# Attention values: rows that neighbouring spans share are loaded once and copied on the chip by GpSimd

## The chip, the cores and the metric

The kernel runs on one core of a Trainium2 chip. A core has five engines with a queue each: TensorE (PE in the profile, its weight loads PEld), VectorE (DVE), ScalarE (ACT), GpSimd (POOL) and SyncE (SP). They run side by side, each takes its own instructions in order, and they wait for one another through semaphores. Sixteen DMA engines move data between the memory of the chip (DRAM) and the core's own memory (SBUF); matmuls write to PSUM. The metric is the device time of one execution in microseconds (us).

## The reference

The program is three layers for 3072 tokens of width 512: chunked attention, a mixture of eight experts of which each token uses two, and a layer that takes the elementwise maximum of three products. Only the first is touched. Per head, it is:

```python
chunk, left_ctx, right_ctx = (32, 16, 8)          # B=4, H=8, S=768, D=64, 8 memory rows
for c in range(S // chunk):
    c_start, c_end = c * chunk, c * chunk + chunk
    k_ctx = k[:, :, max(0, c_start - 16):min(S, c_end + 8)]
    v_ctx = v[:, :, max(0, c_start - 16):min(S, c_end + 8)]
    k_full = np.concatenate([mem_k, k_ctx], axis=2)
    v_full = np.concatenate([mem_v, v_ctx], axis=2)
    scores = scale * np.matmul(q_c, k_full.transpose(0, 1, 3, 2))
    a = np.exp(scores - np.max(scores, axis=-1, keepdims=True))
    a = a / (np.sum(a, axis=-1, keepdims=True) + 1e-09)
    out[:, :, c_start:c_end] = np.matmul(a, v_full)
```

A chunk of 32 queries sees 56 rows of k and v (16 before, its own 32, 8 after) and 8 memory rows. The spans of two neighbouring chunks start 32 rows apart, so they share 24 rows.

## The kernel before

The 3072 tokens are 24 tiles of 128, six for each of the four batches; tile t holds four chunks c. The heads go in four pairs pr. For each tile, v is laid out for the matmul as `vbs[t % NV]` with NV = 3 buffers: partitions 0 to 63 (index a = 0) hold the window of the even head of a pair, partitions 64 to 127 (a = 1) that of the odd head, 56 rows of v and 8 memory rows each; the free dimensions are pair, chunk, and 64 values with a one behind them (D + 1 = 65, so that the product also gives the sum of the weights). The halves of the buffer that belong to the other head are set to zero once, by `clear`. The layout in DRAM (`vw`) is made by `_layout` on the host and has every span in full: a row that two spans share stands there twice.

`load_v(t)` fills the buffer of tile t with two DMAs of the SP queue, one for each a, of 64 rows (56 where the memory rows still stand in the buffer from the tile three before) of 4160 bytes.

The stage runs in steps, written out by `step(t)` for t from -2 to 23. A step holds, in the order in which the engines get them: on even t `load(t + 6)` (k and q of two tiles, from the ACT queue once t + 6 is 6 or more); `scores(t + 2)` on PE; `pv(t)`, the 16 products with v (32 rows of the profile) into `po`; `shift(t + 2)` on DVE (line 369 the maximum, line 372 the subtraction); `expo(t + 2)` on ACT (line 375); `windows(t + 4)`, which spreads k into its spans with two ACT copies (lines 345 and 346) and on two tiles of each batch with two POOL copies (line 350); `ptrans(t + 1)` on PE and its ACT copy (line 383); `xtrans(t - 1)` and its ACT copy (line 409); `gate`; `norm(t)` on DVE with the store of x to `xd` from the SP queue (line 401); and then `load_v(t + 3)` on SP (line 334). So a tile of v is asked for when the product that last read its buffer and the store of that step have been given out, and is used three steps later.

Between these, `pump` deals out the instructions of `route`, the routing of tokens to experts, for groups of tiles. For the first three groups two of its operations run on POOL (lines 444 and 445); DVE takes them up at line 449. At the end of the third group `unit_fetch` lets POOL fetch the first rows for the experts (line 264). From step 19 on, the weights of the experts are split as well (`wsplit`, ACT line 216 and DVE line 213). After step 23 the experts' matmuls begin, which run to the end of the program.

Of the kernel before, what the change touches and what calls it, by code (L numbers as in the profile page):

```python
# [8 lines left out]
F32 = mybir.dt.float32  # L9
# [10 lines left out]
B, H, S, D = 4, 8, 768, 64  # L20
N, DM = B * S, H * D
E, F = 8, 1024
F2 = 768
NT = N // 128
TB = S // 128
HP = H // 2
W = 64
# [9 lines left out]
NV = 3  # L37
# [13 lines left out]
def tile_kernel(ctx, tc, qT, kT, mkT, vw, wgn, noise, w1, w2, m2w, out):  # L51
    nc = tc.nc
    PE, ACT, DVE, POOL, SP = nc.tensor, nc.scalar, nc.vector, nc.gpsimd, nc.sync
# [17 lines left out]
    ld = passing.enter_context(tc.tile_pool(name="ld", bufs=3, side="right"))  # L71
# [14 lines left out]
    def psum(kind, which=None):  # L86
        if which is not None:
            return turns_[kind][which]
        taken[kind] += 1
        return turns_[kind][(taken[kind] - 1) % len(turns_[kind])]  # L90

    def mm(o, l, r, start=True, stop=True):
        PE.matmul(o, l, r, start=start, stop=stop)  # L93

    def spin(o, n, joined=False):

        for i in range(n):
            if n == 10:
                mm(o, ones_r[:, 0:128], ones_r[:, 0:512], start=not joined or i == 0, stop=not joined or i == n - 1)
            else:  # L100
                mm(o, ones, warm, start=(i == 0), stop=(i == n - 1))
# [182 lines left out]
    for e in range(E):  # L284
        n = 512 if e else U0
# [16 lines left out]
    z_all = rt.tile([128, NT, 16], F32, name="z_all")  # L302

    kws = [wk.tile([128, 2, HP, 4, W], F32, name=f"kw{i}", bufs=1) for i in range(2)]
    vbs = [ld.tile([128, 2, HP, 4, D + 1], F32, name=f"v{i}", bufs=1) for i in range(NV)]
    lo, hi = slice(0, 64), slice(64, 128)

    def clear():
# [5 lines left out]
    def load(t):  # L314
        b, i = divmod(t, TB)
        if i == 0:
            m_t[b] = ld.tile([128, HP, 8], F32, name="mk", bufs=2)
            SP.dma_start(m_t[b], mkT[b])
        if i % 2 == 0:
            eng = SP if t < 6 else ACT  # L320
            k_t[t] = ld.tile([128, HP, 280], F32, name="k")
            q_t[t] = ld.tile([128, 2, HP, 128], F32, name="q")
            for j in range(2) if t == 0 else [slice(0, 2)]:
                ks = slice(0, 280) if t else slice(152 * j, 152 + 128 * j)
                eng.dma_start(k_t[t][:, :, ks], kT[b, i // 2, :, :, ks])
                eng.dma_start(q_t[t][:, j], qT[b, i // 2, :, j])
            k_t[t + 1], q_t[t + 1] = k_t[t], q_t[t]

    def load_v(t):
        b, i = divmod(t, TB)  # L330
        n = W if i < NV else 56
        for a in range(2):
            p = slice(64 * a, 64 * a + n)
            SP.dma_start(vbs[t % NV][p, a], vw[b, i, p])

    def windows(t):
        kw = kws[t % 2]
# [14 lines left out]
    sc_t, pp_t, pt_t, po_t, xp_t = {}, {}, {}, {}, {}  # L352
# [32 lines left out]
    def pv(t, pr):  # L385
        if pr == 0:
            po_t[t] = po_b
        o = 2 * (D + 1) * (pr % 2)
        for c in range(4):
            mm(po_t[t][32 * c:32 * c + 32, pr // 2, o:o + 2 * (D + 1)],  # L390
               pt_t[t][:, pr, 32 * c:32 * c + 32], vbs[t % NV][:, :, pr, c, :])

    def norm(t):
        pov = po_t.pop(t)[:, :, 0:4 * (D + 1)].rearrange("p a (h d) -> p a h d", h=4)
# [156 lines left out]
    def pump(n, tensor=True):  # L551

        for r in routes:
            r[1] -= 1
        moved = 1
        while n > 0 and moved:
            moved = 0
            for r in routes[:]:
                if n and r[1] <= 0 and (r[2] not in ("rank", "count", "table") or tensor) and (
                        r[2] != "rank" or r[3] == ranked[0]) and (r[2] != "table" or r is routes[0]):  # L560
                    r[2] = next(r[0], "end")
                    n, moved = n - 1, 1
                    if r[2] == "end":
                        routes.remove(r)
                    elif r[2]:
                        r[1] = hold[0]
# [5 lines left out]
    spin(idle, 12)  # L572
    consts(wk.tile([128, 128], F32, name="dif", bufs=1))
    load_v(0)
    load(2)
    windows(0)
    windows(1)
    clear()
    load_v(1)
    load_v(2)  # L580
    load(4)
    if NV == 4:
# [3 lines left out]
    def turns_of_first():  # L586
        if 0 in fetched:
            turned[0] += 1
            if turned[0] > UH:
                unit_turn(0, turned[1])  # L590
                turned[1] += 1

    def do(f, u, *pr):
        if 0 <= u < NT:
            f(u, *pr)

    def pairs(f, t):
        for pr in range(HP):
            do(f, t, pr)

    def step(t):
        if t + 6 < NT and t % 2 == 0 and t >= 0:
            load(t + 6)
        pairs(scores, t + 2)
        if t <= 0:
            spin(idle, 10 if t < 0 else 6, t == -1)
        pairs(pv, t)
        do(shift, t + 2)
        do(expo, t + 2)
        do(windows, t + 4)  # L610
        pairs(ptrans, t + 1)
        if t < NT - 2:
            pairs(xtrans, t - 1)
            pairs(gate, t - 2)
        turns_of_first()
        pump(PU[1], False)
        do(norm, t)
        if t == NT - 2:
            pairs(gate, t - 2)
            pairs(xtrans, t - 1)  # L620
        if t >= 0:
            do(load_v, t + NV)
        if t < NT - 2:
            pump(PU[2], False)
        else:
            pump(PL)
# [13 lines left out]
    for t in range(-2, NT):  # L640
        step(t)
        if t == WL:
            for _ in range(3):
                wload()
        if t >= WS:
            wsplit(DVE)
        turns_of_first()
# [194 lines left out]
    i = 40  # L842
# [31 lines left out]
    def second(xT, dst, step=lambda s: None, middle=lambda s: None, along=[]):  # L874

        h = [big.tile([128, 2, 512], F32R, name=f"h{i}") for i in range(6)]
        for f in range(3):
            ms = big.tile([128, 2, 512], F32, name=f"h{6 + f % 2}")
            for w in range(3):
                l = quads.pop(3 * f + w)  # L880
                for r in range(2):
# [12 lines left out]
                    if w == 2:  # L894
                        split(m, h[2 * f + r][:, 0, :], h[2 * f + r][:, 1, :], DVE)
        step(18)
        side = spread(along, 24)
        side[4].insert(0, partial(middle, 19))
# [155 lines left out]
    with tc.If(most > CAP):  # L1054
# [10 lines left out]
        with tc.For_i(0, NT // 4, 1) as b:  # L1065
# [3 lines left out]
            for j in range(4):  # L1069
                g = made["cv"].tile([128, 512], F32, name="sq", bufs=1)  # L1070
                SP.dma_start(g, xd[bass.ds(b * 512 + 128 * j, 128), :])
                p = psum("t").rearrange("p (k n) -> p k n", k=HP)
# [4 lines left out]
            for e in range(E):  # L1077
                yp = [misc, tabp, po_b[:, 0], po_b[:, 1]]
                for f in range(8):
# [4 lines left out]
                    p = psum("p")  # L1084
# [17 lines left out]


_INS = [("qT", (B, TB // 2, 128, 2, HP, 128)), ("kT", (B, TB // 2, 128, HP, 280)), ("mkT", (B, 128, HP, 8)),
        ("vw", (B, TB, 128, HP, 4, D + 1)), ("wgn", (DM, 16)), ("noise", (128, NT, E)),
        ("w1", (E, DM, F)), ("w2", (E, F, DM)), ("m2w", (12, 128, 1024))]


def _layout(q, k, v, mem_k, mem_v, moe_w_gate, moe_w_noise, moe_noise, moe_w1, moe_w2,
            moe2_w1, moe2_w2, moe2_w3, moe2_w_out):  # L1110
    import numpy as np
    f = np.float32
    qT = q.reshape(B, HP, 2, TB // 2, 2, 128, D).transpose(0, 3, 2, 6, 4, 1, 5)
    kp = np.zeros((B, H, S + 24, D), f)
    kp[:, :, 16:16 + S] = k
    vp = np.zeros((B, H, S + 24, D), f)
    vp[:, :, 16:16 + S] = v
    kT = np.stack([kp[:, :, 256 * i:256 * i + 280] for i in range(TB // 2)], 1)
    kT = kT.reshape(B, TB // 2, HP, 2, 280, D).transpose(0, 1, 3, 5, 2, 4)
    mkT = mem_k.reshape(B, HP, 2, 8, D).transpose(0, 2, 4, 1, 3)  # L1120
    vw = np.ones((B, TB, 4, HP, 2, W, D + 1), f)
    for i in range(TB):
        for c in range(4):
            o = 128 * i + 32 * c
            vw[:, i, c, :, :, 0:56, 0:D] = vp[:, :, o:o + 56].reshape(B, HP, 2, 56, D)
            vw[:, i, c, :, :, 56:64, 0:D] = mem_v.reshape(B, HP, 2, 8, D)
    vw = vw.transpose(0, 1, 4, 5, 3, 2, 6)
    wgn = np.concatenate([moe_w_gate, moe_w_noise], 1)
    nz = moe_noise.reshape(NT, 128, E).transpose(1, 0, 2)
    wi = np.stack([moe2_w1, moe2_w2, moe2_w3]).reshape(3, 2, 2, 128, 2, 3, 128).transpose(3, 5, 0, 2, 4, 1, 6)  # L1130
    wi = wi.reshape(128, 18, 4, 128)[:, :, [0, 1, 3, 2]]
    wo = moe2_w_out.reshape(2, 3, 128, DM).transpose(2, 1, 0, 3)
    m2w = np.concatenate([wi.reshape(128, 9216), wo.reshape(128, 3072)], 1)
    m2w = np.ascontiguousarray(m2w.reshape(128, 12, 1024).transpose(1, 0, 2)).view(np.int64)
    r = dict(qT=qT.reshape(B, TB // 2, 128, 2, HP, 128), kT=kT.reshape(B, TB // 2, 128, HP, 280),
             mkT=mkT.reshape(B, 128, HP, 8), vw=vw.reshape(B, TB, 128, HP, 4, D + 1), wgn=wgn,
             noise=nz, w1=moe_w1, w2=moe_w2, m2w=m2w)
    return {n: np.ascontiguousarray(r[n]) for n, _ in _INS}

# [14 lines left out]
```

## Time and profile before

| | us |
|---|---|
| median of 3 executions | 1147.58 (1144.96 to 1149.05) |
| the profiled execution | 1145.96 |
| its span, first to last instruction | 1144.1 |
| PE busy in the span | 1106.0 (97%) |
| DVE busy | 632.1 (55%) |
| ACT busy | 391.8 (34%) |
| POOL busy | 215.0 (19%) |

The profile is of one execution. A row names the line of the kernel, the engine, the operation, what it writes and reads, and how often; an idle time is put down to what ended it. PE being busy is a modelled figure, since matmuls are pipelined. The attention takes about the first 135 us of the span; what follows is bound by PE.

### The profile page before, as it was taken

What the parts mean: (1) busy time and instruction counts of PE and PEld (TensorE: products, weight loads), DVE (VectorE), ACT (ScalarE), POOL (GpSimd) and SP (SyncE); (2) the same over time, 40 slices, a digit from 0 to 9 for tenths busy, and PEclk for the clock granted to TensorE, in tenths of its full rate; (3) what the DMA queues carried; (4) which work ended last, traced back from release to release, by engine and by line L of the source; (5) the groups of instructions that cost most, each with busy time, mean ns of one, the idle gap of its engine ahead of it and who ended that gap; (6) DMA issues with size and microseconds to landing.
All of it is one profiled execution on the core that took longest, in us unless ns stands there. A gap on an engine that the chain in (4) does not pass through costs nothing. (4 is left out here: it accounts for less than half of the span.)

```text
span 1144.1 us, 17322 instructions
## 1 busy us (share of the span) xinstructions
PE 1106.0 (97%) x6803; PEld 927.5 (81%) x6804; DVE 632.1 (55%) x1258; ACT 391.8 (34%) x680; POOL 215.0 (19%) x237
## 2 busy tenths in 40 slices
PE   7888899999999999999999999999999999999997
PEld 4777788889888898888888887888877878887886
DVE  4587864363564645755646656334766585655221
ACT  5778423332422523424224332222411152113110
POOL 2001020000011001000110020233456524433000
PEclk9999899999999999999999999999999999999999
DMA  8999533361473544745735675484576635658301
GB/s 242 288 282 302 177 124 107 119 225 62 126 229 111 174 149 142 236 137 167 238 109 162 216 215 183 128 242 158 157 228 218 201 117 170 201 172 281 124 1 40
DMA packets 113689, 199.06 MB, mean 174 GB/s; under 512 B 8576, under 2 KB 46592, under 8 KB 113600
## 3 DMA queue, kind: packets, MB, share of 16 engines
q1 hardware_dynamic: 76736, 109.86, 30.5%
q0 software_dynamic: 34272, 78.13, 22.4%
q10 hardware_dynamic: 2592, 9.88, 2.7%
q8 instruction: 56, 0.92, 0.3%
q14 instruction: 33, 0.27, 0.1%
HBM read 151.18 MB, written 46.66 MB: 173 GB/s over the span
## 5 line engine op out<-in xcount | busy, mean ns | idle before, releaser
L93 PE MATMUL sc<-xT,w 128*128 128x512 f32 (+3 forms) x912 | 193.0, 358 | 5.2 <-DVE h L811 3.8
L93 PE MATMUL pp<-xT,w 128*128 128x512 f32 (+3 forms) x912 | 190.4, 356 | 0.0
L93 PEld LDWEIGHTS sc<-xT,w 128*128 128x128 f32 x912 | 157.0, 188 | 29.0 <-DVE xT L194 3.4
L93 PEld LDWEIGHTS pp<-xT,w 128*128 128x128 f32 x912 | 157.5, 188 | 19.3
L264 POOL DMA_INDIRECT g<-xd,tok x56 | 55.1, 984 | 525.4 <-PE idle L271 242.4
L93 PE MATMUL po<-w,h 128*128 128x512 f32 x548 | 135.0, 395 | 0.0
L93 PE MATMUL misc<-w,h 128*128 128x512 f32 x522 | 127.8, 394 | 0.0
L93 PE MATMUL tabp<-w,h 128*128 128x512 f32 x498 | 121.5, 394 | 0.0
L93 PEld LDWEIGHTS po<-w,h 128*128 128x128 f32 x548 | 101.1, 188 | 20.5
L93 PEld LDWEIGHTS misc<-w,h 128*128 128x128 f32 x522 | 96.5, 188 | 19.8
L93 PEld LDWEIGHTS tabp<-w,h 128*128 128x128 f32 x498 | 92.2, 188 | 18.9
L811 DVE SCALAR_TENSOR_TENSOR h<-sc,h 128x256 fp32r<-128x256 f32 (+2 forms) x96 | 39.8, 443 | 89.0 <-ACT h L807 89.0
L213 DVE TENSOR_TENSOR w<-st,w 128x1024 fp32r<-128x1024 f32 x67 | 81.0, 1217 | 12.5 <-ACT w L216 12.5
L811 DVE SCALAR_TENSOR_TENSOR h<-pp,h 128x256 fp32r<-128x256 f32 (+2 forms) x96 | 39.8, 443 | 72.7 <-ACT h L807 72.7
L807 ACT ACTIVATE h<-sc 128x512 fp32r<-128x512 f32 (+3 forms) x64 | 33.1, 517 | 113.3 <-PE sc L93 106.2
L216 ACT CAST w<-st 128x1024 fp32r<-128x1024 f32 x67 | 70.1, 1047 | 4.1 <-DMA st<-in_w 3.7
L264 POOL DMA_INDIRECT g<-ys,rows x48 | 49.6, 1033 | 102.3 <-DMA ys<-y 62.0
L807 ACT ACTIVATE h<-pp 128x512 fp32r<-128x512 f32 (+3 forms) x64 | 33.1, 517 | 77.5 <-PE pp L93 74.6
L251 ACT CAST top<-val 128x1024 fp32r<-128x1024 f32 x18 | 18.9, 1050 | 79.5 <-DVE val L246 62.7
L194 DVE TENSOR_TENSOR xT<-xp,xT 128x512 fp32r<-128x512 f32 (+1 forms) x35 | 23.3, 665 | 36.5 <-ACT xT L193 36.4
L93 PE MATMUL po<-v,pt 128*32 128x130 f32 x768 | 27.6, 286 | 15.0 <-ACT pt L383 9.3
L193 ACT CAST h<-h 128x128 fp32r<-128x128 f32 (+1 forms) x60 | 18.2, 363 | 66.8 <-DVE h L893 51.7
(197 smaller groups left out, 1571.7 us busy)
## 6 DMA issues: line engine op xcount, KB each, us to landing
st<-in_w SPq DMA_DIRECT2D x64, 512.0 KB, 3.5
w<-m2s POOLq DMA_DIRECT2D x27, 1024.0 KB, 8.2
ys<-y SPq DMA_DIRECT2D x48, 256.0 KB, 3.9
st<-in_m2w SPq DMA_DIRECT2D x24, 512.0 KB, 3.7
m2s<-top SPq DMA_DIRECT2D x18, 512.0 KB, 3.9
m2s<-val SPq DMA_DIRECT2D x18, 512.0 KB
xT<-m2s POOLq DMA_DIRECT2D x9, 1024.0 KB, 6.1
w<-m2s POOLq DMA_DIRECT2D x9, 768.0 KB, 6.7
```

The lines of the kernel that those rows point to most:

```text
L93: PE.matmul(o, l, r, start=start, stop=stop)
L193: ACT.copy(hi, src)
L194: (eng or POOL).tensor_tensor(lo, src, hi.bitcast(F32), op=ALU.subtract)
L213: (eng or POOL).tensor_tensor(w[:, 1, :], st, w[:, 0, :].bitcast(F32), op=ALU.subtract)
L216: return [n, lambda eng: ACT.copy(w[:, 0, :], st), low]
L251: ACT.copy(hi[0], full)
L264: POOL.indirect_dma_start(out=g[0:n], out_offset=None, in_=src, in_offset=bass.IndirectOffsetOnAxis(ap=idx, axis=0))
L807: ACT.activation(h[:, 0, 0:n], p[:, 0:n], AF.Relu)
L811: DVE.scalar_tensor_tensor(o[:, c], p[:, c], 0.0, h[:, 0, c].bitcast(F32), op0=ALU.max, op1=ALU.subtract)
```

## The change

The layout of v becomes chunk first: `vbs` and `vw` have the chunk ahead of the pair. `load_v` now brings rows 0 to 31 of a window for all four chunks, rows 32 to 55 for the last chunk alone, and the memory rows 56 to 63 for all four where they are needed: three DMAs for each a (two where the memory rows stand). A new function `overlap(t)` has POOL copy, for each a, rows 0 to 23 of chunks 1 to 3 to rows 32 to 55 of chunks 0 to 2: 24 partitions of 780 values. It is given out for tile t + 1 at the start of step t, behind `load` and ahead of `scores(t + 2)`. `pv` reads the same values by the new indices.

```diff
-    vbs = [ld.tile([128, 2, HP, 4, D + 1], F32, name=f"v{i}", bufs=1) for i in range(NV)]
+    vbs = [ld.tile([128, 2, 4, HP, D + 1], F32, name=f"v{i}", bufs=1) for i in range(NV)]
...
     def load_v(t):
         b, i = divmod(t, TB)
-        n = W if i < NV else 56
         for a in range(2):
-            p = slice(64 * a, 64 * a + n)
-            SP.dma_start(vbs[t % NV][p, a], vw[b, i, p])
+            for o, n, c in ((0, 32, slice(0, 4)), (32, 24, slice(3, 4)), (56, 8, slice(0, 4)))[0:3 if i < NV else 2]:
+                p = slice(64 * a + o, 64 * a + o + n)
+                SP.dma_start(vbs[t % NV][p, a, c], vw[b, i, p, c])
+
+    def overlap(t):
+
+        for a in range(2):
+            v = vbs[t % NV]
+            POOL.tensor_copy(v[64 * a + 32:64 * a + 56, a, 0:3], v[64 * a:64 * a + 24, a, 1:4])
...
-               pt_t[t][:, pr, 32 * c:32 * c + 32], vbs[t % NV][:, :, pr, c, :])
+               pt_t[t][:, pr, 32 * c:32 * c + 32], vbs[t % NV][:, :, c, pr, :])
...
     def step(t):
         if t + 6 < NT and t % 2 == 0 and t >= 0:
             load(t + 6)
+        do(overlap, t + 1)
         pairs(scores, t + 2)
...
-        ("vw", (B, TB, 128, HP, 4, D + 1)), ("wgn", (DM, 16)), ("noise", (128, NT, E)),
+        ("vw", (B, TB, 128, 4, HP, D + 1)), ("wgn", (DM, 16)), ("noise", (128, NT, E)),
...
-    vw = vw.transpose(0, 1, 4, 5, 3, 2, 6)
+    vw = vw.transpose(0, 1, 4, 5, 2, 3, 6)
```

## Rows read from the trace of the kernel before

**Rows 1.** Busy time by stretch: PE, PEld, DVE, ACT, POOL, granted clock, DMA share, GB/s.

```profile
40.00:60.00 20.00, 18.05 (x375) 16.39 (x368) 11.63 (x29) 16.12 (x26) 1.09 (x4) 1.00 1.00 309
...
120.00:140.00 20.00, 17.89 (x183) 15.87 (x176) 16.88 (x60) 9.68 (x18) 0.00 (x0) 0.86 0.52 165
140.00:1144.00 1004.00, 988.54 (x4755) 828.33 (x4754) 538.08 (x974) 295.82 (x530) 198.18 (x195) 1.00 0.52 162
```

**Rows 2.** PE's waits from 35 to 135 us: total us, times, longest us.

```profile
PE po L93 <- ACT pt L383: 9.3, 10, 1.4
PE po L93 <- DMA v<-in_vw: 1.8, 1, 1.8
```

**Rows 3.** The products with v of tiles 3, 6, 9, 12, 15, 18 (timeline).

```profile
35.17 1.09 PE L93 MATMUL po<-v,pt 128*32 128x130 f32 x32 [0.96 <-ACT pt L383]
...
47.77 1.07 PE L93 MATMUL po<-v,pt 128*32 128x130 f32 x32
...
61.70 1.09 PE L93 MATMUL po<-v,pt 128*32 128x130 f32 x32 [1.42 <-ACT pt L383]
...
75.35 1.09 PE L93 MATMUL po<-v,pt 128*32 128x130 f32 x32 [0.86 <-ACT pt L383]
...
89.10 1.09 PE L93 MATMUL po<-v,pt 128*32 128x130 f32 x32 [0.80 <-ACT pt L383]
...
102.42 1.09 PE L93 MATMUL po<-v,pt 128*32 128x130 f32 x32
```

**Rows 4.** DMA of the stretch 35 to 110 us; issues end with us to landing.

```profile
DMA packets 7653, 22.18 MB, mean 296 GB/s; under 512 B 1326, under 2 KB 1326, under 8 KB 7638
...
v<-in_vw SPq DMA_DIRECT2D x18, 260.0 KB, 7.9
...
k<-in_kT ACTq DMA_DIRECT2D x7, 560.0 KB, 5.9
```

**Rows 5.** The same of the stretch 0 to 400 us: stores of x, loads of q.

```profile
xd<-x SPq DMA_DIRECT2D x24, 256.0 KB, 3.3
...
q<-in_qT ACTq DMA_DIRECT2D x9, 512.0 KB, 6.5
```

**Rows 6.** SP's issues (timeline): first v, last q from SP, v after tile 6.

```profile
4.87 1.15 SPq L334 DMA_DIRECT2D v<-in_vw  x2
...
12.29 0.33 SPq L326 DMA_DIRECT2D q<-in_qT  x1
...
51.00 1.82 SPq L334 DMA_DIRECT2D v<-in_vw  x2
```

**Rows 7.** SP's own waits from 0 to 140 us: total, times, longest.

```profile
SPq L334 <- DMA q<-in_qT: 2.0, 3, 1.1
SPq L326 <- DMA v<-in_vw: 1.2, 1, 1.2
```

**Rows 8.** The issues of v, and ACT's stop before a load of q.

```profile
L334 SPq DMA_DIRECT2D v<-in_vw x48: 314/465/1577, 4.9 to 119.4; - x48
...
L326 ACTq EVENT_SEMAPHORE  x1: 2085/2085/2085, 14.9 to 14.9; - x1
```

**Rows 9.** POOL's operations by form: times, busy us, mean ns.

```profile
L350 POOL COPY kw<-mk 64x128 f32<-64x128 f32 x16 | 4.6, 288 | 35.9 <-PE sc L93 35.0 <-DMA mk<-in_mkT 0.3
...
L311 POOL MEMSET v<- 64x1040 f32 x3 | 2.9, 959 | 0.2
```

**Rows 10.** Routing between POOL and DVE, first and third group (timeline).

```profile
58.13 0.28 POOL L444 TENSOR_TENSOR a<-a,nz 128x48 f32<-128x48 f32 x1 [23.12 <-ACT a L440]
...
58.81 0.31 DVE L449 MAX8 top<-a 128x8 f32<-128x8 f32 x3 [0.22 <-POOL a L445]
...
91.20 0.62 DVE L424 TENSOR_TENSOR rc<-iota_j,co 128x448 f16<-128x448 f16 x1
...
91.43 0.48 POOL L444 TENSOR_TENSOR a<-a,nz 128x24 f32<-128x24 f32 x1 [2.41 <-DVE a L442]
```

**Rows 11.** ACT's later wait for k at the start (timeline).

```profile
23.19 0.94 ACT L345 COPY kw<-k 64x896 f32<-64x896 f32 x1 [3.12 <-DMA k<-in_kT]
```

More of the change, by code (lines that the diff above doesn't have):

```diff
@@ L1135, in _layout @@
     r = dict(qT=qT.reshape(B, TB // 2, 128, 2, HP, 128), kT=kT.reshape(B, TB // 2, 128, HP, 280),
-             mkT=mkT.reshape(B, 128, HP, 8), vw=vw.reshape(B, TB, 128, HP, 4, D + 1), wgn=wgn,
+             mkT=mkT.reshape(B, 128, HP, 8), vw=vw.reshape(B, TB, 128, 4, HP, D + 1), wgn=wgn,
              noise=nz, w1=moe_w1, w2=moe_w2, m2w=m2w)
```

## The prediction

> **What bounds the kernel now.** I read the stretches first [rows 1]. From 140 us on PE is busy for 988.5 of 1004 us, and the change touches nothing there: what it gains or costs must show as an earlier or later start of that part, so only the first 135 us count. There the DMA engines look full (share 1.00 at 309 GB/s from 40 to 60 us), which invites the reading that v's bytes set the pace. The second view, PE's waits [rows 2], says otherwise: in 100 us PE waited 9.3 us for the transposed weights from ACT and once, 1.8 us, for v. The pace is a loop through PE, DVE and ACT, three steps of which take 12.6 us (tiles 3 to 6), 13.65 (9 to 12) and 13.3 (15 to 18) [rows 3]. Loads keep up, but only just: v lands 7.9 us after its issue [rows 4], it is issued about 3.2 us after its buffer's last product starts (47.77 to 51.00 us [rows 3, 6]), so a tile is ready some 11.5 us after that start where 13 are allowed: about 1.6 us of slack.
>
> **A turn of eight.** SP's waits [rows 7] hold some that no data explains: a load of v waits for a load of q, a load of q for a load of v. The start shows the pattern [rows 6]: v's first two loads are SP's 8th and 9th issue, and the load of q at 12.29 us, the 17th, is released by v's landing, eight issues after the 9th. I take it that the loads and stores of SP and ACT share eight semaphores in turn, each waiting until the one eight before has landed. ACT is in this turn too: its queue stopped 2.09 us before a load of q [rows 8]. Today a step has four of these DMAs (a store, two of v, one of k or q on average), so the one eight before is two steps old, about 9 us, against landings of 3.3 to 7.9 us [rows 4, 5].
>
> **The change part by part.** *Bytes.* Each half tile loses 24 rows of three chunks, 24 x 3 x 1040 B = 75 KB of 266 or 233 KB. The stretch from 35 to 110 us has 32 half tiles, so 2.4 of its 22.18 MB go [rows 4], 10.8%. As nothing waits there, I count the relief at zero by itself; if bytes did set the pace it would be 0.108 x 75 = 8.1 us.
>
> How much relief each DMA engine sees is open. The Trainium skill, "DMA: Bandwidth & Descriptors", section "Why a DMA increments its semaphore by 16 and not by 1", says that a load spreads over the largest number of engines up to 16 that divides its rows, the lowest ones: 24 rows over 12, 8 rows over 8. By an estimate from that page the busiest engines go from four rows to three and a half for a half tile, a relief of an eighth and not of 28%; no row here shows the engines one by one.
>
> *Issues.* v takes 48 issues now. Twelve tiles will take six and twelve take four, 120 in all; 72 more at 0.465 us [rows 8] are 33 us of SP's time over some 24 steps, which SP has (six are 2.8 us of a step of 4.4). SP's time itself costs nothing; the place in the turn does. On steps t that load a tile with memory rows (3 to 5, 9 to 11, 15 to 17, the three heavy groups) a step has a store, six of v and a share of k and q: 3 + 18 + 2 = 23 DMAs in three steps. With eight in flight and a landing time L, 23 of them take 23 / 8 x L. L has two ends: 3.3 us, a store of x [rows 5], gives 9.5 us, under the 13 that three steps take anyway and hence nothing; 7.9 us, today's v [rows 4], gives 22.7, that is 9.5 us more in each group. The new pieces are smaller and the queue a little emptier, but they share it with loads of k and q that take 5.9 and 6.5; I take 5.5, between v's and the store's. 23 / 8 x 5.5 = 15.8 us, against 12.6, 13.65 and 13.3 [rows 3]: 3.2 + 2.2 + 2.5 = 7.9 us. The light groups (20 in three steps, 13.75 us, where tiles 6 to 9 and 12 to 15 take 13.9 and 13.75 now [rows 3]) don't bind. Behind SP's waiting issue stand the next pieces, the store of x and the next tile's v; behind ACT's, the exponentials of the step.
>
> *POOL copies.* 48 copies of 24 partitions x 780 values. The trace has no such copy. Bounds: the fill of 1040 values took 0.96 us, 0.92 ns a value, so 0.72 us; the copy of 128 took 0.288 us, 2.25 ns a value with its start, so 1.76 us [rows 9]. I take 1.3, nearer to the copy with part of its time as start. The copy of the first half runs while the second half is still landing, so one copy lies behind the last row that it needs, and before that the pieces of the second half that follow in the queue are done with. Against that, the last row needed comes about 1 us sooner, since less precedes it. The slack of 1.6 us goes to this (1.3 us, and SP's later issue of the second half, three issues of 0.465 instead of one, 0.9 us, less the 1 us). So I let slack and copies cancel, and charge the turn in full.
>
> *POOL's order.* `overlap(t + 1)` waits on POOL for v. Behind it stand, in the same step, routing's two operations (lines 444, 445), which took their turn at once before (DVE waited 0.22 us [rows 10]), the copies of k's memory rows, which have a step to spare, and once the fetch for the experts. v becomes ready late in a step, so in the three routed groups DVE, which takes its instructions in order, may stand up to 2.5 us at line 449; part of it falls into waits that DVE has anyway. I take 1 us each, 3 us together (0 to 7.5). The fetch at step 19 is delayed by at most a copy or two, in a stretch where DVE and ACT split weights; zero.
>
> A second contention can be seen in one row: the operation on 24 columns took 0.48 us on POOL while DVE ran line 424 with two inputs from SBUF, and the one on 48 columns took 0.28 [rows 10]. The Trainium skill, "SBUF — State Buffer", section "Who interferes with whom", has the rule: a DVE instruction with two SBUF inputs and a POOL instruction that reads SBUF exclude each other for the whole instruction; the trace agrees, with those 0.48 us ending 0.1 us after line 424 ends. By the row, a copy may wait 0.6 us or a routing operation 1.3 us, a few times in a group; I leave it inside the 0 to 7.5.
>
> *Start.* ACT waits 3.1 us for the third pair's k [rows 11]. Less of v lies ahead of it (six half tiles, 0.45 MB less, at 250 GB/s some 1.8 us), but with eighteen issues of v instead of six that k is issued later by the turn. I take 1 us of gain, between 2 of gain and 1.5 of loss.
>
> *PE.* The same matmuls with the same shapes; zero. If PE idles more, its clock may fall, as it has at 120 to 140 us (0.86 [rows 1]); up to 2 us, in the range.
>
> **Sum.** 7.9 + 3 - 1 = 9.9 us; a part of POOL's stalls falls on steps that the turn holds up anyway (the third routed group, at 91 us, on step 15 [rows 3, 10]), where one hides the other, so I take 8.5. Against the profiled execution: 1145.96 + 8.5 = 1154.5. That execution lies 1.6 us under the median of the three, so as a median 1156.
>
> **The rivals.** (A) *The turn doesn't bind*: pieces land within 4.5 us, 23 / 8 x 4.5 = 12.9 us, what three steps take. Then POOL's stalls less the start remain, -1 to +3 us: about 1148.5. For it: landings of 3.3 us where the queue is light; against: a DMA share of 1.00. (B) *The bytes do set the pace*, unseen because the loop adapts to late loads: 8.1 us from the stage and 1 to 2 from the start: about 1138. For it: the full share, and slack of only 1.6 us; against: a single wait of PE for v. It decides if the steps get shorter than 4.3 us. (C) *Every tile late*: L stays at 7.9, or copies take 1.8 us each with SP's issues late on all steps: 9.5 us x 3 groups = 28 us, 1176. (D) The change doing something else than it says I hold out: the diff moves the bytes it names.
>
> A change within 0.3% (3.4 us) can't be told from none here. Chances: forecast (steps 4 to 18 us longer) 0.52, A 0.22, B 0.16, C 0.10. B is the faster side, most of it beyond 3.4 us; A is mostly same, with a little of each side: faster 0.17, same 0.23, slower 0.60. The forecast's own range is 1151 to 1165. For eight in ten it must take in A and part of B and C: 1143 to 1170.
>
> **What would show it.** Right: SP's waits on loads and stores grow from a few us to tens; heavy groups take 15 to 17 us for three steps, light ones as before; PE's waits in front of the products name POOL or v; DVE waits at line 449. Wrong: three steps of a heavy group still in 13.5 us (A), under 12.5 (B), or SP never waiting for a landing (no turn); POOL copies under 0.7 or over 1.8 us would move the slack sum by as much.

## The result, and the profile after

| | before | after |
|---|---|---|
| median, us | 1148.32 (6 executions) | 1159.09 (6 executions) |
| ratio | | 1.0088 (95% interval 1.0064 to 1.0113) |
| the profiled execution, us | 1145.96 | 1154.89 |
| its span, us | 1144.1 | 1153.0 |

The change costs 0.88%, some 10 us. The profiled execution after is the fastest of its six, so the rows below show 8.9 of these 10 us. In the code after, the copies are line 340, the loads of v still line 334, and what stood behind them is six lines further down (line 383 is now 389, 401 is 407, 449 is 455).

First the stretches, with the columns of [rows 1]:

```profile
20.00:40.00 20.00, 11.52 (x219) 9.93 (x208) 7.42 (x17) 11.00 (x16) 5.08 (x9) 0.83 0.71 226
40.00:60.00 20.00, 17.31 (x325) 15.62 (x324) 9.82 (x22) 15.56 (x23) 6.86 (x9) 0.91 0.75 225
...
140.00:1153.00 1013.00, 999.07 (x4860) 838.21 (x4860) 549.00 (x1010) 301.41 (x540) 200.14 (x195) 1.00 0.52 162
```

From 40 to 60 us the DMA engines went from full at 309 GB/s [rows 1] to three quarters at 225. The bytes are fewer, and yet the tiles come later: the engines are not what is short. The last part is PE's as before. The products with v, as in [rows 3], for tiles 1, 3, 6, 9, 12, 15, 18 and 23:

```profile
28.05 2.04 PE L93 MATMUL po<-v,pt 128*32 128x130 f32 x32 [7.48 <-issue]
...
37.68 1.22 PE L93 MATMUL po<-v,pt 128*32 128x130 f32 x32 [1.00 <-issue]
...
50.53 1.07 PE L93 MATMUL po<-v,pt 128*32 128x130 f32 x32
...
66.20 1.17 PE L93 MATMUL po<-v,pt 128*32 128x130 f32 x32 [1.05 <-ACT pt L389]
...
81.25 1.31 PE L93 MATMUL po<-v,pt 128*32 128x130 f32 x32 [1.83 <-POOL v L340]
...
98.27 1.09 PE L93 MATMUL po<-v,pt 128*32 128x130 f32 x32
...
114.02 1.31 PE L93 MATMUL po<-v,pt 128*32 128x130 f32 x32
...
142.67 1.92 PE L93 MATMUL po<-v,pt 128*32 128x130 f32 x32
```

The same rows of before for the first and the last of them:

```profile
25.80 1.17 PE L93 MATMUL po<-v,pt 128*32 128x130 f32 x32 [2.91 <-issue]
...
130.87 1.86 PE L93 MATMUL po<-v,pt 128*32 128x130 f32 x32
```

Against before [rows 3], tile 1 is 2.3 us late, tile 3 2.5, tile 6 2.8, tile 9 4.5, tile 12 5.9, tile 15 9.2, tile 18 11.6, tile 23 11.8. The span ends 8.9 us later, so the part behind the attention gives 2.9 us back. The delay has two places: the start (2.3 us by tile 1), and the steps from tile 6 to tile 18 (8.8 us). Where the start lost is in ACT's row that answers to [rows 11], and in SP's issues that answer to [rows 6]:

```profile
25.45 0.94 ACT L351 COPY kw<-k 64x896 f32<-64x896 f32 x1 [6.68 <-DMA k<-in_kT]
```

```profile
9.85 7.93 SPq L334 DMA_DIRECT2D v<-in_vw  x12
17.82 0.35 SPq L325 DMA_DIRECT2D k<-in_kT  x1
```

The k of tiles 4 and 5 is issued at 17.82 us, behind twelve pieces of v that took 7.93 us to give out, instead of at 10.63. ACT waits 6.7 us for it. PE stands idle 7.5 us before tile 1; its row names no releaser, and that it stands behind ACT is read from the order in time. For the later steps, SP's own waits from 0 to 150 us (total, times, longest), as in [rows 7]:

```profile
SPq L334 <- DMA k<-in_kT: 13.4, 7, 4.6
...
SPq L334 <- DMA q<-in_qT: 6.6, 7, 1.5
...
SPq L407 <- DMA k<-in_kT: 4.0, 1, 4.0
```

Loads of v and a store of x wait for loads of k and q with which they share no data: 24.6 us with the smaller rows of that list, where before had 5.8. One of these waits in SP's and ACT's timelines:

```profile
49.02 0.35 ACTq L325 DMA_DIRECT2D k<-in_kT  x1
...
50.23 0.37 SPq L407 DMA_DIRECT2D xd<-x  x1
53.68 3.11 SPq L334 DMA_DIRECT2D v<-in_vw  x6
```

SP has given out its store at 50.6 us and could go on: the product that last read the buffer of this tile ended at 47.9. The load of v goes out at 53.68, when the k that ACT gave out at 49.02 has landed. POOL is idle 59.1 us for v, PE 3.5 us for POOL's copies:

```profile
L340 POOL COPY v<-v 24x780 f32<-24x780 f32 x48 | 41.7, 869 | 67.4 <-DMA v<-in_vw 59.1 <-PE xp L412 4.3 <-DMA g<-xd,tok 2.9
```

```profile
PE po L93 <- issue: 10.2, 4, 7.5
PE po L93 <- ACT pt L389: 5.8, 5, 1.5
PE po L93 <- POOL v L340: 3.5, 3, 1.8
```

A copy takes 0.83 us. Routing waits once where the prediction looked for it, 1.7 us:

```profile
DVE top L455 <- POOL a L451: 1.7, 1, 1.7
```

### The profile page after: what moved, and what is told of

It reads as the page before. It is cut to its first block, busy times and chain, and to the rows that moved or that the text cites. A ratio compares the mean times of both kernels' runs of the same rounds, so it can differ in the third digit from the quotient of the medians.

```text
span 1153.0 us, 17523 instructions
## 1 busy us (share of the span) xinstructions
PE 1110.3 (96%) x6804; PEld 932.6 (81%) x6804; DVE 637.1 (55%) x1258; ACT 392.5 (34%) x680; POOL 259.7 (23%) x285
## 5 line engine op out<-in xcount | busy, mean ns | idle before, releaser
L340 POOL COPY v<-v 24x780 f32<-24x780 f32 x48 | 41.7, 869 | 67.4 <-DMA v<-in_vw 59.1
L93 PE MATMUL po<-v,pt 128*32 128x130 f32 x768 | 32.7, 308 | 23.2 <-issue 10.2
L93 PEld LDWEIGHTS po<-v,pt 128*32 128x32 f32 x768 | 25.7, 121 | 28.3 <-issue 17.6
```

Of the source, the lines that this page charges most:

```text
L340: POOL.tensor_copy(v[64 * a + 32:64 * a + 56, a, 0:3], v[64 * a:64 * a + 24, a, 1:4])
```

## The experiments

The theory is that of the prediction, called T: the loads and stores of SP and ACT take a small set of semaphores in turn, and 72 more of them make each wait for the landing of an earlier one. The rivals are P, the copies behind the landing; R, routing's operations behind the copies on POOL; and the mere number of transfers, or SP's time to issue them. Each kernel was timed beside the kernel before; the ratio and its 95% interval are not exactly the quotient of two medians. "SP's waits for k and q" are the sums over the view of SP's waits in the first 160 us.

**Cut loads alone, all bytes.** The kernel before with this:

```diff
-        n = W if i < NV else 56
         for a in range(2):
-            p = slice(64 * a, 64 * a + n)
-            SP.dma_start(vbs[t % NV][p, a], vw[b, i, p])
+            for o, n in ((0, 32), (32, 24), (56, 8))[0:3 if i < NV else 2]:
+                p = slice(64 * a + o, 64 * a + o + n)
+                SP.dma_start(vbs[t % NV][p, a], vw[b, i, p])
```

> The kernel before (median 1148.3 us) with its loads of v cut at rows 32 and 56 as the changed kernel cuts them: the same bytes as before, no copies, 120 loads of v instead of 48. Theory T (the loads and stores of SP and ACT take eight semaphores in turn, so the number of them sets a pace): 8 to 14 us slower, about 1158, with the first product of tile 1 some 2 us later and SP waiting for landings of k and q for tens of us in the first 140 us. Theory P (the copies of POOL, which come behind the landing, are what makes tiles late): no difference, 1147 to 1150. Theory R (routing's operations stand on POOL behind the copies): no difference.

Measured: 1.0159 (1.0126 to 1.0191), 1168.16 us. Slower than the changed kernel, without any copy: P and R are not needed for the loss. SP waits 48.7 us for k and q:

```profile
SPq L334 <- DMA k<-in_kT: 25.8, 8, 5.2
...
SPq L401 <- DMA k<-in_kT: 10.1, 2, 5.7
```

**Copies alone.** The changed kernel with whole loads:

```diff
-            for o, n, c in ((0, 32, slice(0, 4)), (32, 24, slice(3, 4)), (56, 8, slice(0, 4)))[0:3 if i < NV else 2]:
-                p = slice(64 * a + o, 64 * a + o + n)
-                SP.dma_start(vbs[t % NV][p, a, c], vw[b, i, p, c])
+            p = slice(64 * a, 64 * a + (W if i < NV else 56))
+            SP.dma_start(vbs[t % NV][p, a], vw[b, i, p])
```

> The changed kernel with whole loads of v (48, the bytes of before) and with its POOL copies, which write the values that the loads brought already. T: within 0 to 3 us of before, 1148 to 1151, since the turn is that of before; what is added is a copy behind each landing. P: 1156 to 1160, as slow as the changed kernel. R: part of it, 1150 to 1153, with DVE waiting at the routing's first operation after POOL.

Measured: 1.0019 (0.9997 to 1.0042), 1152.18 us. All 48 copies behind whole landings cost 0 to 0.4%. P as the main cause falls. R is not ruled out at this size: DVE waits 1.8 us in two waits at the operation that takes up routing behind POOL (line 454).

**Cut loads with the saving, no copies.**

```diff
-            POOL.tensor_copy(v[64 * a + 32:64 * a + 56, a, 0:3], v[64 * a:64 * a + 24, a, 1:4])
+            if t < NV:
+                POOL.memset(v[64 * a + 32:64 * a + 56, a, 0:3], 0.0)
```

> The changed kernel with its 120 short loads and without the POOL copies: rows 32 to 55 of the first three chunks' windows are set to zero once and stay so, that part of the attention is left out. T: 1154 to 1158, nearly as slow as the changed kernel (1159.1). P: 1147 to 1150, as before. R: 1154 to 1157, less what DVE waits at routing.

Measured: 1.0080 (1.0056 to 1.0103), 1157.44 us. The changed kernel without its copies is as slow as with them, within the intervals. The loss sits in the loads.

**Tiny loads on SP, and on POOL.** The kernel before with three loads of 64 x 16 bytes in each tile, 72 in all, which bring nothing that is used:

```diff
+    tiny = ld.tile([64, NT, 3, 4], F32, name="tiny", bufs=1)
...
             SP.dma_start(vbs[t % NV][p, a], vw[b, i, p])
+        for j in range(3):
+            SP.dma_start(tiny[:, t, j], vw[b, i, 0:64, j, 0, 0:4])     # POOL.dma_start in the second kernel
```

> The kernel before with three more loads on SP behind v's two in each of the 24 tiles: 72 in all, each 64 rows of 16 bytes into a tile that nobody reads (74 KB in all, so no bytes to speak of). T: 5 to 12 us slower, about 1156, though nothing waits for what they bring: only their place in the turn and SP's time to issue them count. P and R: 1147 to 1150. If it is slower, but SP's waits are not for landings, SP's issue time would be the cause and not the turn.

> The kernel before with the same 72 tiny loads as in the run with them on SP (which took 1.06% more than before), but given out by POOL, whose loads count on semaphores of their own. T (the turn of eight of SP and ACT): 0 to 2 us slower, 1149 to 1151, from POOL's issue time alone. If the mere number of transfers on the DMA engines were the cost, it would be as slow as on SP, about 1161.

Measured: on SP 1.0106 (1.0065 to 1.0146), 1161.14 us; on POOL 1.0022 (1.0009 to 1.0034), 1150.97 us. Loads without bytes, copies or readers cost as much as the whole change when SP gives them out, and a fifth of it from POOL: not their number on the DMA engines counts, but where they are queued. Nor did they slow v's own transfers: from 35 to 110 us the loads of 64 rows landed 4.7 us after their issue in the mean, 7.0 in the kernel before (by the marks on the semaphores, told with the table below). In the trace of the one on SP, the loads of v (line 335) wait for k, and PE for v:

```profile
SPq L335 <- DMA k<-in_kT: 11.1, 4, 6.1
```

```profile
PE po L93 <- DMA v<-in_vw: 11.4, 3, 5.3
```

With the tiny loads on POOL the first of these rows is 0.6 us in 2 waits. The Trainium skill, "DMA: Bandwidth & Descriptors", section "Issuing engines are not separate DMA queues", says that issuing from several engines saves only the sequencer's time for the issue. Here the move saved about 10 us; the waits in the rows show why, since the issues of this program also wait for landings, and POOL's not for the same ones: in the traces' records of the issues, SP's and ACT's DMAs all count on the semaphores 101, 102, 104, 105, 106, 108, 109 and 110, and POOL's on 111 to 118.

**Fewer cut tiles.** Whole loads on the twelve tiles that bring memory rows, cut loads and copies on the other twelve:

```diff
+            if i < NV:
+                p = slice(64 * a, 64 * a + W)
+                SP.dma_start(vbs[t % NV][p, a], vw[b, i, p])
+                continue
-            for o, n, c in ((0, 32, slice(0, 4)), (32, 24, slice(3, 4)), (56, 8, slice(0, 4)))[0:3 if i < NV else 2]:
+            for o, n, c in ((0, 32, slice(0, 4)), (32, 24, slice(3, 4))):
...
-        for a in range(2):
+        for a in range(2 if t % TB >= NV else 0):
```

> The changed kernel with whole loads on the tiles that bring memory rows (no copies there) and cut loads with copies on the other twelve tiles: 72 loads of v instead of 48 or 120, and 38% of the saving in bytes. T: at most 4 DMAs a step on one half of the steps and 6 on the other, 20 in three steps, which the turn just carries: 0 to 4 us slower than before, 1149 to 1153. A cost in proportion to the loads added (24 of 72) would give 3.3 us, a cost in proportion to the copies 5 us.

Measured: 0.9995 (0.9975 to 1.0015), 1149.26 us. The cost is not in proportion to the loads added: 24 more cost nothing, 72 more 0.9%. The bytes saved on twelve tiles may pay for a part of the 24. A limit between 20 and 23 DMAs in three steps would look like this, but this run alone doesn't show that it is the count; the landings below speak against it.

**The order at the start.** One line moved, in the kernel before and in the changed one:

```diff
+    load(4)
     load_v(1)
     load_v(2)
-    load(4)
```

> The kernel before with one line moved: k and q of tiles 4 and 5 are asked for ahead of v of tiles 1 and 2. ACT waits 3.1 us for that k at 23.2 us in the kernel before, and tiles 1 and 2 have 6 and more us in hand. T for the start (the order in the turn and in the queue decides when k comes): 2 to 3 us faster, about 1146.5, with the first product of tile 1 at 23 to 24 us instead of 25.8. If other waits stand right behind: no difference.

> The changed kernel with one line moved: k and q of tiles 4 and 5 are asked for ahead of v of tiles 1 and 2, so 12 loads of v no longer stand before them in the turn. The changed kernel lost 2.3 us at tile 1, where ACT waits 6.7 us for that k. T: the start comes back and more, 3 to 5 us faster than the changed kernel, about 1154.5 or 0.5% over before; the 6 to 9 us of the later steps stay. If the start's wait only moves to the v of tile 1: no difference, 0.9% over before.

Measured: before with k first 0.9975 (0.9956 to 0.9994), 1146.34 us, tile 1 at 20.94 us. The changed kernel with k first 1.0151 (1.0119 to 1.0184), 1167.85 us: the expectation failed. The first part of it held, tile 1 starts at 22.85 us instead of 28.05, but by tile 3 over two fifths of it are gone, by tile 4 all of it, and by tile 18 it is 12.5 us behind the changed kernel:

```profile
22.85 1.32 PE L93 MATMUL po<-v,pt 128*32 128x130 f32 x32 [1.75 <-POOL v L340]
...
34.73 2.03 PE L93 MATMUL po<-v,pt 128*32 128x130 f32 x32 [4.69 <-POOL v L340]
...
126.55 1.17 PE L93 MATMUL po<-v,pt 128*32 128x130 f32 x32 [0.62 <-issue]
```

SP's waits and one stretch of its timeline say where it went. The moved line changed nothing after the start but the place of every DMA in the turn:

```profile
SPq L334 <- DMA k<-in_kT: 38.3, 12, 6.5
```

```profile
45.58 10.10 SPq L334 DMA_DIRECT2D v<-in_vw  x6
```

Six issues of v took 10.1 us. This also decides between the turn and SP's issue time: both kernels issue the same DMAs, and so spend the same issue time, yet SP waits 46.9 us for k and q in one and 24.6 in the other, and the one with more is 0.6% slower.

**Short pieces from POOL.** The changed kernel, with rows 0 to 31 on SP and the rest on POOL; then with k first as well; then all bytes in pieces so, without copies:

```diff
-                SP.dma_start(vbs[t % NV][p, a, c], vw[b, i, p, c])
+                (SP if o == 0 else POOL).dma_start(vbs[t % NV][p, a, c], vw[b, i, p, c])
```

> The changed kernel with its short pieces (24 rows of one chunk, 8 memory rows) given out by POOL instead of SP: SP has two loads of v a tile, as before, so the turn is that of before, and the bytes are fewer. T: the turn no longer costs; 1147 to 1153, if POOL itself keeps up. Against it: POOL's queue then holds two or four issues of about 0.8 us and two copies of 0.83 us a step, and its issues stand behind copies that wait for landings; if that binds, 1155 and more, with PE's waits naming POOL's copies or the pieces.

> The short pieces on POOL (0.27% faster than before) and k and q of tiles 4 and 5 first (0.25% faster by itself). If the two gains were of different places they would add to 0.5%, about 1143.5. The trace of the one with the pieces on POOL shows its first product of tile 1 at 21.3 us already, as early as the one with k first (20.9), so I expect no more than either alone: 0.2 to 0.3% under before, 1146.

> The kernel before with its loads of v cut as in the changed kernel, all bytes, no copies; rows 0 to 31 from SP, the other pieces from POOL. Beside the run with the pieces on POOL and the copies (0.27% under before) it tells what the bytes are worth: T with the bytes at nothing: as before or a little under, 1146 to 1150, since the copies are gone too. If the bytes saved are what made that run faster: 2 to 4 us slower than it, 1148.5 to 1151, with the start as in the kernel before (tile 1 at 25 to 26 us).

Measured: 0.9973 (0.9960 to 0.9985), 1146.04 us; with k first 0.9958 (0.9936 to 0.9979), 1146.31 us; all bytes without copies 1.0022 (1.0002 to 1.0042), 1153.57 us. The change as such, bytes saved and copies on POOL, is a gain once its extra loads leave SP: 1.2% lie between it and the changed kernel. SP's waits for k and q fall to 2.1 us. The third kernel carries the bytes that the first one saves, and has no copies; their intervals don't meet, half a per cent apart. A part of that may be the longer pieces that POOL gives out there, which was not tried by itself.

**The best of these.** The kernel with fewer cut tiles, its 24-row piece on POOL, and k first:

```diff
-                SP.dma_start(vbs[t % NV][p, a, c], vw[b, i, p, c])
+                (SP if o == 0 else POOL).dma_start(vbs[t % NV][p, a, c], vw[b, i, p, c])
...
+    load(4)
     load_v(1)
     load_v(2)
-    load(4)
```

> Whole loads on tiles with memory rows, the saving and the copies on the other twelve with their short piece on POOL, and k and q of tiles 4 and 5 first: the turn of before, 38% of the saving, 24 copies. T: the gain of the start without the stalls that POOL makes late in the stage: 0.3 to 0.5% under before, 1143.5 to 1146. If POOL's copies cost as much on twelve tiles as on all: 0.2% under, as k first alone.

Measured: 0.9951 (0.9929 to 0.9973), 1144.41 us. It is faster than both kernels, by 0.5% and 1.4%; against the two above with k first or pieces on POOL alone it can't be told apart for sure.

**All of them in one table**, by SP's waits for landings of k and q. The last column is counted from the semaphores that the traces' records give for each DMA: how many of SP's DMAs take over the semaphore of a k or q of ACT when at most four other DMAs of SP and ACT were given out in between.

| kernel | SP's waits for k and q, us | ratio to before | SP's DMAs close behind a k or q |
|---|---|---|---|
| short pieces on POOL | 2.1 | 0.9973 | 0 |
| copies alone | 4.2 | 1.0019 | 0 |
| before | 5.8 | 1 | 0 |
| tiny loads on POOL | 8.1 | 1.0022 | 0 |
| short pieces on POOL, k first | 8.5 | 0.9958 | 0 |
| all bytes, pieces on POOL | 9.5 | 1.0022 | 0 |
| fewer cut tiles, POOL, k first | 12.3 | 0.9951 | 0 |
| before, k first | 12.4 | 0.9975 | 0 |
| fewer cut tiles | 15.1 | 0.9995 | 0 |
| tiny loads on SP | 18.5 | 1.0106 | 2 |
| the changed kernel | 24.6 | 1.0088 | 7 |
| no copies | 28.5 | 1.0080 | 6 |
| changed, k first | 46.9 | 1.0151 | 12 |
| cut loads, all bytes | 48.7 | 1.0159 | 13 |

Up to 15 us of waits the kernels lie within half a per cent of before, either way. Above it all five are slow: the three with 18 to 29 us can't be told apart, and the two near 48 are slower than the changed kernel.

The last column says how the turn comes to cost so much. In the kernel before, SP takes over a place of ACT's k or q 9.5 us after that load was given out (the median of 14, at least 7.0), when it has mostly landed. In the changed kernel SP is through the turn sooner: the median of 16 is 5.3 us, the least 3.9, about the time that these loads take to land. The last column goes with the cost in all fourteen kernels; since the waits themselves shift what is given out when, this is a reading of the records and not shown by an experiment of its own.

The same records give the landings, which the view shows for some loads only: a DMA has landed with the last mark on its semaphore before the next DMA takes it over. Means over the DMAs given out from 35 to 110 us:

| | before, us | after, us |
|---|---|---|
| v, whole: 64 rows, 56 rows | 7.0, 5.7 | |
| v, pieces: 32, 24, 8 rows | | 3.7, 3.1, 3.3 |
| store of x | 5.4 | 4.4 |
| k | 5.0 | 4.4 |
| q | 7.4 | 6.0 |
| under way at once, of eight | 5.6 | 5.4 |

The transfers of the changed kernel land sooner and not later, and the eight places are no fuller than before. In the slower changed kernel with k first only 3.8 are taken in the mean. All eight are taken at the start, up to 15 us. In the four later waits of over 2 us for a k (they end at 53.6, 65.2, 86.0 and 93.7 us) 4, 2, 2 and 6 were under way just before the end: SP stood at the one place whose k had not landed while others were free.

## Why the prediction was right, and where its steps were not

**The total and the cause held.** Forecast 8.5 us, 1156 us; measured about 10, 1159, as the forecast's own case. SP waits in a turn of eight for landings of loads with which it shares no data, as forecast. The loads' number, with no byte, no copy and no reader, reproduces it (tiny loads on SP); whole loads with all the copies don't.

**The distribution did not.** The prediction put 7.9 us into the three heavy groups themselves. By the rows, tiles 3 to 6 lost 0.3 us, 9 to 12 1.4, 15 to 18 2.4: 4.1 in all. The groups called light lost 1.7 (6 to 9) and 3.3 (12 to 15), and tiles 18 to 21 0.7. A tile is used three steps after its load is given out, so what SP loses while tiles 6 to 8 are loaded may fall on the steps that use them; no row ties the two together.

**The size of the turn's term was right by luck.** It was 23 / 8 x L with L at 5.5 us, as if eight places were always full. Measured, the DMAs given out while the three heavy groups of tiles (6 to 8, 12 to 14, 18 to 20) are loaded land in 4.3, 3.3 and 4.0 us in the mean; 23 / 8 x L is then 9.6 to 12.3 us, less than three steps take anyway, and the sum would have had nothing there. That is the condition of rival A, pieces that land within 4.5 us, and the turn cost its 10 us all the same. The formula treats all eight places as alike. They are not: what counts is how soon behind a k or q SP comes to that load's place, and the prediction had this reading in its own paragraph on the turn (before, the one eight back is two steps old, about 9 us) but did not carry it into the sum: with 23 in three steps the one eight back is one step old. The k-first run of the changed kernel shows it: with the same DMAs, the order alone decided over 22 us of SP's waiting and 0.6% of the time. The two ends of L were off as well, since the view tells only some landings: 7.9 us for v and 3.3 for a store, where all of those in the stretch give 5.7 to 7.0 and 5.4.

**The start had the wrong sign.** Forecast 1 us gained (2 gained to 1.5 lost), measured 2.3 us lost at tile 1. The term weighed fewer bytes against a later issue and took the bytes for more. In the experiment on the start, the place of the k in the order alone moved tile 1 by 4.9 us. The row of the issue moved from 10.63 to 17.82 us, and ACT's wait from 3.1 to 6.7.

**POOL's copies** were taken as 1.3 us and took 0.83, close to the lower bound of 0.72 by the fill: this copy of one run of 780 values goes at about the rate of the fill. The copy of 128 values in [rows 9], in 16 short runs, was the poorer neighbour; why was not tried. That the copies cancel against the slack held: alone they cost 0.19%, with an interval that reaches zero.

**POOL's order** was taken as 3 us and showed one wait of 1.7 us on DVE. The contention with DVE that the third group hinted at [rows 10] is there and small: a routing operation that took 0.63 us before (first row) took 1.20 beside two copies that took 2.00 instead of 1.72.

```profile
72.80 0.63 DVE L424 TENSOR_TENSOR rc<-rc,ids 128x448 f16<-128x448 f16 x1
...
103.26 2.00 POOL L340 COPY v<-v 24x780 f32<-24x780 f32 x2
103.37 1.20 DVE L430 TENSOR_TENSOR rc<-rc,ids 128x448 f16<-128x448 f16 x1
```

The Trainium skill, "SBUF — State Buffer", section "Who interferes with whom", has such a pair exclude each other for the whole instruction; both rows are longer, as that has it, though the routing operation lost 0.57 us where some 0.7 of the first copy were still to run.

**The bytes at zero** was an error that the total hid. It followed from PE waiting once for v; but with the turn out of the way the kernel that saves the bytes is 0.27% faster than before, copies included, and 0.5% (5.6 us) faster than its neighbour with all bytes. On SP too, cut loads with all bytes took 0.7% more than the changed kernel. The first product of tile 1 shows a part of it, 25.80 us before; here with all bytes and the pieces on POOL, with the bytes saved too, and in the kernel before with k first:

```profile
23.44 1.09 PE L93 MATMUL po<-v,pt 128*32 128x130 f32 x32 [2.65 <-DMA q<-in_qT]
...
21.25 1.17 PE L93 MATMUL po<-v,pt 128*32 128x130 f32 x32 [1.01 <-ACT pt L389]
...
20.94 1.09 PE L93 MATMUL po<-v,pt 128*32 128x130 f32 x32 [0.36 <-ACT pt L383]
```

So about half of the earlier start goes with the bytes, and the order of the loads alone can bring as much. Rival B, that the bytes set the pace, was about half right, and only where the turn doesn't bind.

**What stays open.** That the turn has eight places is in the records; no run changed their number. In order of issue two DMAs of one semaphore are not always eight apart (5 to 11 before, 2 to 14 after), since SP and ACT give theirs out at their own times; who stands close behind whom was counted, and apart from the moved line no run changed it by itself. How the waits of SP add up to the lateness of each tile was not followed. The clock granted to PE from 35 to 110 us fell from 1.00 to 0.93 with the stalls, and to 0.84 in the changed kernel with k first; how much of each loss is the clock and how much the wait before it was not separated.

## What to carry to other kernels

Cutting a load into pieces to save bytes spends something else: each piece takes a place among the transfers that may be under way at once, and in a program whose issues wait for earlier landings the pieces can cost more than the bytes bring. Look for waits in the DMA queue's own view that no data explains. Then ask not only how many transfers a step has, but how soon the queue comes round to the place of a long load that another engine gave out, and compare that with the landing of this load. Give the small pieces to a queue that doesn't take part. Where a place in such a turn is shared by long and short loads, moving one line at the start can change which short load waits for which long one in every later step.

## What the runs showed of the hardware that was not expected

A GpSimd copy of 24 partitions with a shift of 32 partitions ran at 0.83 us for 780 values, 1.07 ns a value, near the 0.92 of a plain fill [rows 9]. And three loads of 64 x 16 bytes a tile from GpSimd's queue cost 0.22% (0.09 to 0.34) in all, where 72 of them from SP's cost 1.06%. In this program's records POOL's DMAs count on semaphores of their own, and SP's and ACT's share eight.
